# One scheduler task of six products where the second MLP layer had two tasks of three

## The chip, the cores and the metric

The kernel runs on one core of one Trainium2 chip. A core has a matrix engine (PE, with its weight loads listed apart as PEld), a vector engine (DVE), a scalar engine (ACT), a general engine (POOL) and a sequencer that mostly issues transfers (SP). Each engine works through its own instructions in the order in which they were written down, and waits for the others through semaphores. The metric is the time of one execution on the device in microseconds.

## The reference

Three stages follow each other. The attention works on 4 batches of 8 heads with 576 tokens of 64 numbers, under a mask of 64-token blocks. Its result is read as 2304 tokens of 512 numbers and goes through a two-layer MLP whose inner function is a leaky ramp with its own slope for each of 2048 hidden units. Then each token goes to one of 8 experts.

```python
x = attn_out.transpose(0, 2, 1, 3).reshape(2304, 512)
h = x @ w_in                                  # 512 -> 2048
g = np.maximum(h, 0.0) + alpha * np.minimum(h, 0.0)
y = g @ w_out                                 # 2048 -> 512
expert = np.argmax(y @ w_gate, axis=1)        # one of 8
out[mask] = gate_w[mask, None] * (np.maximum(y[mask] @ w1[e], 0.0) @ w2[e])
```

## The kernel before

All large products are made from numbers split into a high and a low part, so one product of the mathematics is three on PE: high by high, high by low and low by high.

**Attention** is cut into 16 pairs of heads (`pair`), each pair into 5 chunks of tokens (`unit`). For each chunk PE makes the scores `S`; DVE finds their maxima (`nb`, L428); ACT makes the exponentials `P` (L442); DVE their sums (`sm`, L449 and L450); POOL or DVE multiplies `P` by them (L477); PE transposes `P` into `PT` (L465); ACT or DVE copies that to `F` (L470); PE multiplies `F` with the values into `o` (L499), and the result goes to memory as `xT`. A pair begins with the transposes `tr` of its queries and keys (L340, L342), which ACT and DVE turn into `qhi`, `qlo`, `khi`, `klo` (L353 to L377). `tr`, `PT` and `o` of later pairs take turns in two PSUM buffers called `PT`, so a transpose waits until the readers of the one before the last are through.

**The first MLP** goes through the tokens in 9 groups of 256 (`Mlp1.plan`). For each of 16 slices `f` of the hidden units, `l1` makes 12 products of 256 columns into `l` (L578); DVE applies the ramp (`t`, L582 and L583), ACT casts the high part (`gh`, L586), POOL or DVE takes the low part (`gl`, L589). `l2` adds that slice into the two accumulators of the group, one for each 128 tokens, `acc` 0 and `acc` 1: three products of 512 columns each, `gh` by the high weights, `gh` by the low weights, and `gl` by the high weights (L609). When all 16 slices are in, ACT copies both accumulators to `y` (L620), and `route_plan` finds the expert of each token: transposes `rt`, products `lg`, a rank by the product `rk` (L723, L724), eleven small DVE operations that end in `ig` (L744), and two scatters of `info` that POOL issues one after the other (L747).

**Weights** of this MLP arrive as 64-bit numbers and are turned into high and low parts on the fly: ACT scales (L245), POOL takes the sign (L248), DVE puts the bits together (L251, L252), then the high part is cast (L256) and the low part is a difference (L260). While the last group runs, the weights of the first expert are loaded and split in the same way (`first_expert`, L1251 and L1256). The experts follow; the change does not touch them.

**What sets the order.** Attention, weights, MLP and routing are all tasks of one list scheduler (`Plan`). `order` simulates the engines with a duration given for each task. At each step it looks at all tasks whose inputs are there, takes those that can start within 100 ns of the earliest, and of these the one with the lowest priority number. A buffer is taken by the first task that uses it. The tasks' bodies are then written down in that order, and nothing reorders them later. `l1` and `l2` have numbers from 100000 up; attention has 0 to 16000, so attention goes first wherever both can start.

Of the kernel before, what the change touches and what calls it, by code (L numbers as in the profile page):

```python
# [18 lines left out]
P = 128  # L19
# [6 lines left out]
GT = 2  # L26
# [187 lines left out]
def cols(n):  # L214

    return max(n / 2.4 + 12, 108)
# [306 lines left out]
class Mlp1:  # L523
# [72 lines left out]
        
    def l2(A, pl, g, f):
        nc = A.nc
        for i in range(GT):
            acc = ("acc", g, i)  # L600
            if f == 0:
                pl.buf(acc, "H")
            c = slice(P * i, P * i + P)

            def second(on, i=i, c=c, acc=acc):
                wh, wl = (A.W["o", f][:, z] for z in range(2))
                gh, gl = pl["gh", g, f], pl["gl", g, f]
                for j, (x, w) in enumerate(((gh, wh), (gh, wl), (gl, wh))):
                    nc.tensor.matmul(pl[acc], lhsT=x[:, c], rhs=w, start=f == 0 and j == 0, stop=f == 15 and j == 2)  # L609

            pl.add(("PE", 3 * cols(512)), second, A.W1.names(("o", f)) + [("gh", g, f), ("gl", g, f)], [acc, ("l2", g, f)], 100000 + 100 * (16 * g + f + 1) + 20 + i)

    def fins(A, pl, g):
        nc = A.nc
# [208 lines left out]
class Experts:  # L823
# [132 lines left out]
    def tile128(A, n, W, it, x, step, aheads):  # L956
# [29 lines left out]
        step(1)  # L986
        Y = A.psp.tile("H", f"Y{n}")
        l2((0, 1))
        turn(1)
        aheads()  # L990
        step(7)
        l2(range(2, 8))
        nc.scalar.activation(A.yo[0], Y, AF.Copy, scale=it[:, 0, 1:2].bitcast(F32))
        A.scatter(A.yo[0], it)

    def tile64(A, n, W, it, x, step, aheads):
# [36 lines left out]
        for i in range(1, 4):  # L1033
# [3 lines left out]
            nc.scalar.copy(A.s, H)  # L1037
        Y = [A.psp.tile("H", f"Y{n}_{h}")[:, 0:256] for h in range(2)]
        l2(0, range(4))
        turn(3)  # L1040
        step(8)
# [290 lines left out]
```

## Time and profile before

| | us |
|---|---|
| median of 3 runs | 1041.59 |
| the three runs | 1037.69 to 1044.52 |
| profiled execution | 1040.76 |
| its span, first to last instruction | 1039.0 |
| PE busy | 934.6 (90% of the span) |
| DVE busy | 524.6 |
| ACT busy | 417.0 |
| POOL busy | 360.8 |

The span can be read in stages. Up to about 160 us attention, weight preparation and the first group run together, with DVE nearly as busy as PE. From there to about 519 us attention and MLP groups are interleaved, and PE is busy almost throughout. To about 716 us the MLP runs alone, and the experts end the kernel. PE has two clock levels, 2.4 GHz and 1.2 GHz; the profile lists the granted share (1.00 and 0.50). Matmuls are pipelined: the distance from one start to the next tells their cost better than their listed duration, which is longer. In the timeline a row merges equal instructions that follow each other; a bracket at its end holds the engine's idle time just before it and what ended it.

### The profile page before, as it was taken

How to read it: one execution, taken by the hardware profiler on the slowest of the kernel's cores; microseconds unless marked ns; L12 is line 12 of the kernel's file. 1: busy time of each engine (PE TensorE's matmuls, PEld its weight loads, DVE VectorE, ACT ScalarE, POOL GpSimd, SP SyncE). 2: the span in 40 equal slices, each digit the busy share in tenths (PEclk: the TensorE clock that was granted, in tenths of full speed). 3: DMA queues.
4: the chain of work that ended last, by engine and by line, in shares of the span. 5: the costliest groups of instructions: out<-in, count | busy, mean ns of one | idle time of the engine just before them, and what ended most of it. 6: DMA issues, size and time to landing. Idle time of an engine off the chain costs nothing. (4 is left out here: it accounts for less than half of the span.)

```text
span 1039.0 us, 18700 instructions
## 1 busy us (share of the span) xinstructions
PE 934.6 (90%) x6725; PEld 809.6 (78%) x6725; DVE 524.6 (50%) x1286; ACT 417.0 (40%) x1131; POOL 360.8 (35%) x429
## 2 busy tenths in 40 slices
PE   7884979999999999999999999998799999988554
PEld 6653868788788878888899999987688888877543
DVE  4898989554655645645443434455224314415130
ACT  5785554444544545545422121224124224325231
POOL 3556866332332333343322222232114212315030
PEclk8795998999899999999999999999999999999776
DMA  6553721112310121300010010033245212506110
GB/s 185 165 196 123 223 87 34 34 47 67 82 47 19 54 67 47 87 19 13 14 41 25 18 41 1 22 83 121 80 154 172 94 44 86 178 27 205 30 36 6
DMA packets 85296, 79.78 MB, mean 77 GB/s; under 512 B 53759, under 2 KB 65679, under 8 KB 85136
## 3 DMA queue, kind: packets, MB, share of 16 engines
q1 hardware_dynamic: 73984, 57.37, 19.0%
q0 software_dynamic: 4240, 11.56, 3.4%
q10 hardware_dynamic: 6912, 8.92, 2.4%
q8 instruction: 77, 1.26, 0.5%
q14 instruction: 83, 0.68, 0.2%
HBM read 63.49 MB, written 14.72 MB: 75 GB/s over the span
## 5 line engine op out<-in xcount | busy, mean ns | idle before, releaser
L578 PE MATMUL l<-xh,wi 128*128 128x256 f32 x1152 | 236.3, 290 | 1.9 <-DVE t L583 1.8
L578 PEld LDWEIGHTS l<-xh,wi 128*128 128x128 f32 x1152 | 191.6, 195 | 7.9 <-DVE t L583 2.7
L609 PE MATMUL acc<-wo,gh 128*128 128x512 f32 x576 | 191.7, 414 | 0.0
L578 PE MATMUL l<-xl,wi 128*128 128x256 f32 x576 | 165.3, 287 | 0.7 <-DVE xl L557 0.7
L589 POOL TENSOR_TENSOR gl<-t,gh 128x256 fp32r<-128x256 f32 x119 | 91.6, 770 | 193.9 <-ACT gh L586 163.0
L477 POOL TENSOR_SCALAR P<-P,sm 128x256 f32<-128x256 f32 (+4 forms) x89 | 102.2, 1152 | 162.4 <-DVE sm L450 70.2
L582 DVE TENSOR_SCALAR t<-l,al 128x256 f32<-128x256 f32 x144 | 69.5, 482 | 158.2 <-PE l L578 146.0
L586 ACT CAST gh<-t 128x256 fp32r<-128x256 f32 x144 | 58.5, 407 | 173.2 <-DVE t L583 75.5
L609 PE MATMUL acc<-wo,gl 128*128 128x512 f32 x288 | 113.9, 396 | 4.9 <-POOL gl L589 4.9
L578 PEld LDWEIGHTS l<-xl,wi 128*128 128x128 f32 x576 | 112.2, 195 | 4.6 <-DVE xl L557 1.3
L609 PEld LDWEIGHTS acc<-wo,gh 128*128 128x128 f32 x576 | 95.7, 190 | 16.1 <-issue 5.2
L465 PE MATMUL PT<-ident,P 128*128 128x128 f32 (+1 forms) x400 | 72.8, 297 | 27.3 <-DVE qlo L360 12.8
L470 ACT COPY F<-PT 128x256 f32<-128x256 f32 (+3 forms) x154 | 61.2, 415 | 74.3 <-PE PT L465 72.5
L465 PEld LDWEIGHTS PT<-ident,P 128*128 128x128 f32 (+1 forms) x400 | 48.7, 148 | 44.6 <-POOL P L477 10.9
L428 DVE TENSOR_REDUCE nb<-S 128x1 f32<-128x256 f32 (+4 forms) x160 | 70.9, 476 | 23.3 <-PE S L415 21.3
L499 PE MATMUL o<-F,v 128*64 128x128 f32 (+2 forms) x960 | 70.4, 279 | 2.3 <-ACT F L470 2.0
L609 PEld LDWEIGHTS acc<-wo,gl 128*128 128x128 f32 x288 | 54.3, 189 | 19.2 <-POOL gl L589 7.0
L442 ACT ACTIVATE P<-S,nb 128x128 f32<-128x128 f32 (+3 forms) x128 | 67.0, 532 | 5.6 <-DVE nb L428 3.0
L927 POOL DMA_INDIRECT out_dram<-yo,it x21 | 22.7, 1082 | 133.8 <-ACT yo L953 68.4
L499 PEld LDWEIGHTS o<-F,v 128*64 128x64 f32 (+1 forms) x960 | 50.0, 145 | 19.2 <-ACT F L470 5.5
L583 DVE SCALAR_TENSOR_TENSOR t<-l,t 128x256 f32<-128x256 f32 x144 | 61.1, 425 | 5.0
L880 DVE TENSOR_TENSOR e<-raw,e 128x512 fp32r<-128x512 f32 x44 | 39.8, 928 | 33.0 <-ACT e L879 33.0
(351 smaller groups left out, 1758.3 us busy)
## 6 DMA issues: line engine op xcount, KB each, us to landing
raw<-in_moe_w_dram SPq DMA_DIRECT2D x80, 256.0 KB
rawi<-in_moe_w_in_dram SPq DMA_DIRECT2D x16, 512.0 KB
rawo<-in_moe_w_out_dram SPq DMA_DIRECT2D x16, 512.0 KB
xr<-xT SPq DMA_DIRECT2D x9, 512.0 KB
v<-in_v_dram SPq DMA_DIRECT2D x32, 128.0 KB
x<-y ACTq DMA_DIRECT2D x16, 256.0 KB
xT<-xo ACTq DMA_DIRECT2D x16, 160.0 KB
q<-in_q_dram SPq DMA_DIRECT2D x20, 128.0 KB
```

The costliest lines, as they stand in the source:

```text
L428: nc.vector.tensor_reduce(pl["nb", p, c][:, j:j + 1], pl[Ss[j]][:, 0:N[j]], axis=AX.X, op=ALU.max, negate=True)
L442: nc.scalar.activation(pl[x][:, 0:N[j]], pl[Ss[j]][:, 0:N[j]], AF.Exp, bias=nb, scale=1.0, accum_out=pl["sm", p, c][:, j:j + 1])
L465: nc.tensor.transpose(pl[t][0:w, k], pl[x][:, P * k:P * k + w], A.K.ident)
L470: f(pl[F][:, 0:n], pl[t][:, 0:n])
L477: (nc.gpsimd if on == "POOL" else nc.vector).tensor_scalar(y, y, pl["sm", p, c][:, jj:jj + 1], None, op0=ALU.mult)
L499: nc.tensor.matmul(pl[o][r, 0:N], lhsT=v[0:w, 2 * kc + h], rhs=f, start=kc == 0, stop=kc == c, skip_group_check=True)
L578: nc.tensor.matmul(pl[l][:, 0:G], lhsT=a[:, c], rhs=b, start=k == 0 and j == 0, stop=k == 3 and j == 2)
L582: nc.vector.tensor_scalar(pl[t], x, 0.0, A.K.al[:, f:f + 1], op0=ALU.min, op1=ALU.mult)
L583: nc.vector.scalar_tensor_tensor(pl[t], x, 0.0, pl[t], op0=ALU.max, op1=ALU.add)
L586: nc.scalar.copy(pl[gh], pl[t])
L589: (nc.gpsimd if on == "POOL" else nc.vector).tensor_sub(pl[gl], pl[t], pl[gh].bitcast(F32))
L609: nc.tensor.matmul(pl[acc], lhsT=x[:, c], rhs=w, start=f == 0 and j == 0, stop=f == 15 and j == 2)
```

## The change

`l2` gave the scheduler two tasks for each slice, one for each half of the group's tokens; now it gives it one task that does the six products of both halves in a row. Products, operands, accumulators and their order within a slice stay the same. Both accumulators are now taken by the first such task of a group.

```diff
     def l2(A, pl, g, f):
         nc = A.nc
-        for i in range(GT):
-            acc = ("acc", g, i)
-            if f == 0:
+        accs = [("acc", g, i) for i in range(GT)]
+        if f == 0:
+            for acc in accs:
                 pl.buf(acc, "H")
-            c = slice(P * i, P * i + P)
-
-            def second(on, i=i, c=c, acc=acc):
-                wh, wl = (A.W["o", f][:, z] for z in range(2))
-                gh, gl = pl["gh", g, f], pl["gl", g, f]
+
+        def second(on):
+            wh, wl = (A.W["o", f][:, z] for z in range(2))
+            gh, gl = pl["gh", g, f], pl["gl", g, f]
+            for i, acc in enumerate(accs):
                 for j, (x, w) in enumerate(((gh, wh), (gh, wl), (gl, wh))):
-                    nc.tensor.matmul(pl[acc], lhsT=x[:, c], rhs=w, start=f == 0 and j == 0, stop=f == 15 and j == 2)
-
-            pl.add(("PE", 3 * cols(512)), second, A.W1.names(("o", f)) + [("gh", g, f), ("gl", g, f)], [acc, ("l2", g, f)], 100000 + 100 * (16 * g + f + 1) + 20 + i)
+                    nc.tensor.matmul(pl[acc], lhsT=x[:, P * i:P * i + P], rhs=w, start=f == 0 and j == 0, stop=f == 15 and j == 2)
+
+        pl.add(("PE", 6 * cols(512)), second, A.W1.names(("o", f)) + [("gh", g, f), ("gl", g, f)], accs + [("l2", g, f)], 100000 + 100 * (16 * g + f + 1) + 20)
```

Since one choice of the scheduler shifts all that follow, the order of the whole first 716 us differs from slice 7 of the first group on; before that point, and in the experts, it is the same. Of the 144 pairs of halves, 52 had other work between their halves; now none has. Stretches of other work (attention, routing) that stand between MLP tasks on PE are 153 after 167. Attention now reaches into the sixth group, where it ended with the fifth.

PE, slice 8 of the first group (`acc_0`, `acc_1` are the halves, `o_1` a chunk's product with the values). Before:

```order
L609 MATMUL acc_0_1521<-wo_1700,gh_8_1797 128x512 x2
L609 MATMUL acc_0_1521<-wo_1700,gl_8_1821 128x512
L499 MATMUL o_1_1860<-F_1_0_1817,v_1158 64x128
L499 MATMUL o_1_1860<-F_1_1_1844,v_1158 64x128
L499 MATMUL o_1_1860<-F_1_0_1817,v_1158 64x128
L499 MATMUL o_1_1860<-F_1_1_1844,v_1158 64x128
L609 MATMUL acc_1_1531<-wo_1700,gh_8_1797 128x512 x2
L609 MATMUL acc_1_1531<-wo_1700,gl_8_1821 128x512
```

And now:

```order
L609 MATMUL acc_0_1521<-wo_1700,gh_8_1797 128x512 x2
L609 MATMUL acc_0_1521<-wo_1700,gl_8_1821 128x512
L609 MATMUL acc_1_1525<-wo_1700,gh_8_1797 128x512 x2
L609 MATMUL acc_1_1525<-wo_1700,gl_8_1821 128x512
L499 MATMUL o_1_1867<-F_1_0_1817,v_1158 64x128
L499 MATMUL o_1_1867<-F_1_1_1844,v_1158 64x128
L499 MATMUL o_1_1867<-F_1_0_1817,v_1158 64x128
L499 MATMUL o_1_1867<-F_1_1_1844,v_1158 64x128
```

The halves stand together, and the attention product moves behind both.

DVE, a little later, about 150 us into the span before (`stw` and `wi` belong to the weights, `nb`, `nbb`, `P_3_1`, `qlo` and `klo` to attention). Before:

```order
L252 SCALAR_TENSOR_TENSOR stw_1988<-rawi_2_137,stw_1988 128x512
L428 TENSOR_REDUCE nb_4_2002<-S_4_1_1981 128x1
L433 TENSOR_TENSOR nbb_2027<-nb_4_2002 128x1
L360 SCALAR_TENSOR_TENSOR qlo_2029<-tr_0_1993,qhi_2014 128x512
L260 TENSOR_TENSOR wi_2_2018<-stw_1988,wi_2_2018 128x512
L362 TENSOR_TENSOR klo_2045<-tr_1_2005,khi_2023 128x512
L251 SCALAR_TENSOR_TENSOR stw_2034<-rawi_3_138,stw_2034 128x512
L252 SCALAR_TENSOR_TENSOR stw_2034<-rawi_3_138,stw_2034 128x512
```

And now:

```order
L252 SCALAR_TENSOR_TENSOR stw_1988<-rawi_2_137,stw_1988 128x512
L477 TENSOR_SCALAR P_3_1_1964<-P_3_1_1964,sm_3_1962 128x512
L428 TENSOR_REDUCE nb_4_2002<-S_4_1_1981 128x1
L260 TENSOR_TENSOR wi_2_2017<-stw_1988,wi_2_2017 128x512
L251 SCALAR_TENSOR_TENSOR stw_2024<-rawi_3_138,stw_2024 128x512
L252 SCALAR_TENSOR_TENSOR stw_2024<-rawi_3_138,stw_2024 128x512
L433 TENSOR_TENSOR nbb_2037<-nb_4_2002 128x1
L360 SCALAR_TENSOR_TENSOR qlo_2039<-tr_0_1993,qhi_2019 128x512
```

`qlo` has four more operations ahead of it: the scaling of `P_3_1`, which POOL did before, and three of the weights. `klo` goes far back.

POOL, around the scatters of the third group's routing, which run among the first slices of the fourth group (`gl_2` and `gl_3` are that group's; `q8hi`, `q8lo` are cleared for the next pair). Before:

```order
L477 TENSOR_SCALAR P_4_1_4819<-P_4_1_4819,sm_4_4809 128x320
L739 TENSOR_SCALAR ig_4888<-pid 128x2
L589 TENSOR_TENSOR gl_2_4905<-t_2_4867,gh_2_4897 128x256
L747 DMA info<-ig_4888,si_4883 18432x2 x2
L382 MEMSET q8hi_4970 64x64 x2
L382 MEMSET q8lo_4973 64x64 x2
L589 TENSOR_TENSOR gl_3_4990<-t_3_4948,gh_3_4979 128x256
```

And now:

```order
L739 TENSOR_SCALAR ig_4800<-pid 128x2
L477 TENSOR_SCALAR P_2_0_4759<-P_2_0_4759,sm_2_4760 128x384
L589 TENSOR_TENSOR gl_2_4823<-t_2_4770,gh_2_4788 128x256
L747 DMA info<-ig_4800,si_4795 18432x2 x2
L589 TENSOR_TENSOR gl_3_4865<-t_3_4837,gh_3_4845 128x256
L477 TENSOR_SCALAR P_3_1_4879<-P_3_1_4879,sm_3_4870 128x512
```

The low part of slice 3 stands directly behind the scatters, and a long scaling behind that. The routings of the fourth and fifth groups have this piece again.

## Rows read from the trace of the kernel before

**Rows 1.** Windows: length, busy us (count) of PE, PEld, DVE, ACT, POOL, PE clock, DMA.

```profile
240.00:280.00 40.00, 38.82 (x313) 32.33 (x310) 22.64 (x79) 20.97 (x72) 12.12 (x22) 0.87 0.28 75
360.00:400.00 40.00, 38.43 (x306) 32.64 (x304) 20.53 (x65) 17.81 (x59) 15.98 (x25) 0.96 0.19 44
560.00:600.00 40.00, 40.00 (x266) 36.68 (x266) 17.60 (x51) 8.87 (x22) 11.27 (x15) 1.00 0.09 27
680.00:720.00 40.00, 36.04 (x229) 32.19 (x227) 21.79 (x49) 13.28 (x29) 13.97 (x16) 1.00 0.42 116
```

**Rows 2.** Timeline of PE: start us, length us; halves of slices, whole and split.

```profile
125.50 0.61 PE L609 MATMUL acc<-wo,gh 128*128 128x512 f32 x2
126.19 0.61 PE L609 MATMUL acc<-wo,gh 128*128 128x512 f32 x2
...
226.10 0.73 PE L609 MATMUL acc<-wo,gh 128*128 128x512 f32 x2
...
226.99 0.50 PE L413 MATMUL S<-khi,qhi 64*128 64x512 f32 x2
...
227.91 0.73 PE L609 MATMUL acc<-wo,gh 128*128 128x512 f32 x2
...
228.71 0.49 PE L465 MATMUL PT<-ident,P 128*128 128x128 f32 x3
```

**Rows 3.** Timeline of PE, the stall of the first group and what follows.

```profile
154.38 2.29 PE L465 MATMUL PT<-ident,P 128*128 128x128 f32 x8 [3.82 <-DVE qlo L360]
...
159.70 0.58 PE L578 MATMUL l<-xh,wi 128*128 128x256 f32 x1
```

**Rows 4.** Timeline of DVE ahead of and behind `qlo`.

```profile
152.19 0.48 DVE L428 TENSOR_REDUCE nb<-S 128x1 f32<-128x320 f32 x1
...
153.55 0.68 DVE L360 SCALAR_TENSOR_TENSOR qlo<-tr,qhi 128x512 fp32r<-128x512 f32 x1
154.15 0.68 DVE L260 TENSOR_TENSOR wi<-stw,wi 128x512 fp32r<-128x512 f32 x1
...
155.35 0.68 DVE L251 SCALAR_TENSOR_TENSOR stw<-rawi,stw 128x512 int32<-128x512 int32 x1
156.06 1.41 DVE L252 SCALAR_TENSOR_TENSOR stw<-rawi,stw 128x512 int32<-128x512 int32 x1
```

**Rows 5.** Groups of instructions by line and shape: busy us, mean ns.

```profile
L477 DVE TENSOR_SCALAR P<-P,sm 128x512 f32<-128x512 f32 x17 | 9.1, 546 | 0.6
```

**Rows 6.** Windows as in Rows 1, three stretches at the lower clock.

```profile
153.20:163.40 10.20, 8.91 (x51) 7.84 (x52) 9.96 (x16) 5.87 (x15) 7.49 (x10) 0.50 0.26 59
259.00:269.30 10.30, 9.74 (x48) 8.30 (x49) 7.75 (x33) 4.81 (x15) 2.71 (x3) 0.50 0.22 64
375.10:378.50 3.40, 3.40 (x15) 3.12 (x13) 0.33 (x2) 1.15 (x5) 1.16 (x2) 0.50 0.09 13
```

**Rows 7.** Timeline of PE, fourth group, from the rank to slice 3.

```profile
361.12 0.38 PE L724 MATMUL rk<-oh,U 128*128 128x16 f32 x2
...
373.51 0.51 PE L609 MATMUL acc<-wo,gl 128*128 128x512 f32 x1 [1.22 <-POOL gl L589]
```

**Rows 8.** Timeline of POOL in the same stretch: the scatters, and slice 3.

```profile
365.30 1.06 POOL L747 DMA_INDIRECT info<-ig,si  x1 [1.35 <-DVE ig L744]
370.97 0.96 POOL L747 DMA_INDIRECT info<-ig,si  x1 [4.61 <-DMA info<-ig,si]
...
372.74 0.72 POOL L589 TENSOR_TENSOR gl<-t,gh 128x256 fp32r<-128x256 f32 x1
```

**Rows 9.** The scatters' line, all 18 of them.

```profile
DMA to landing us min/median/max: 3.3/3.6/5.4
```

**Rows 10.** Timeline of PE, an `l` block's starts, and the ninth group's stall.

```profile
120.31 0.40 PE L578 MATMUL l<-xh,wi 128*128 128x256 f32 x2
120.55 0.28 PE L578 MATMUL l<-xl,wi 128*128 128x256 f32 x1
...
686.86 0.50 PE L609 MATMUL acc<-wo,gl 128*128 128x512 f32 x1 [2.39 <-POOL gl L589]
```

**Rows 11.** Timelines of ACT and PE where the MLP ends.

```profile
715.12 2.19 ACT L1251 CAST e<-raw 128x512 fp32r<-128x512 f32 x4
...
722.34 1.27 PE L683 MATMUL rt<-ident,raw 128*128 128x128 f32 x8 [3.91 <-ACT raw L630]
```

**Rows 12.** The line of the accumulators' copies: who waited for it.

```profile
ACT F L470: 0.4, 1
```

## The prediction

> **What bounds the kernel now.** I read the windows first, 40 us at a time. Where the MLP runs alone PE is busy 40.00 of 40 us at full clock, with DVE, ACT and POOL under half; where attention is mixed in, it is busy 38.4 to 38.8 [rows 1]. PE is therefore the bound from about 160 us on, and a reordering that keeps its work can win only what PE loses: idle stretches, stretches at the lower clock, and whatever a change of work on PE costs. The timeline of PE shows few losses after 150 us. There is one wait of 3.82 us for `qlo` in the first group [rows 3]; waits of 1 to 2.4 us for a low part `gl` [rows 7, 10]; one of 3.91 us at the end of the MLP [rows 11]; and stretches at half clock, two of about 10 us and two of 3.4 us, of which the second stands at 463.8 and looks as the first [rows 6]. With half of the low-clock time all of it is about 26 us, 2.5% of the whole. The DVE timeline tells what the wait for `qlo` was [rows 4], the POOL timeline what the low parts waited for [rows 8].
>
> **The change, part by part.** Nothing is added or removed: all 864 products of L609 stay. What moves is the order, so each term below is a place where PE loses time, before and now.
>
> *Fewer changes of work on PE.* Whole halves start 126.19 - 125.50 = 0.69 us apart. A half that gives way to scores takes 226.99 - 226.10 = 0.89, and one that follows them 228.71 - 227.91 = 0.80 [rows 2]. So a stretch of other work costs 0.2 us where PE goes over to it and 0.1 where it comes back; for transposes I found nearer 0.1 in all. The order has 153 such stretches after 167, 14 fewer: at 0.1 to 0.3 each 1.4 to 4.2 us. I take **-3.0**; the ends are 0 (the pieces meet other expensive neighbours) and 52 split pairs by 0.2, -10.
>
> *The wait for `qlo`.* PE's transpose at 154.38 waits until DVE has read `tr` [rows 3]. In the order after DVE has four more operations ahead: the scaling of `P_3_1`, 0.55 us by the mean of its kind [rows 5], a low part, 0.68, and the two bit operations, 0.71 from start to start and 1.41 [rows 4]. That is 3.35 us. Some of the 1.36 us between 152.19 and 153.55 was itself waiting (the maximum takes 0.48), which the new operations fill: up to 0.8 comes off. `qlo` and the transpose are late by 2.5 us at best guess, and PE idles 6.3 instead of 3.82. What was queued behind it changes too: before, 5.3 us of attention at half clock followed, up to 159.70; now four `l` blocks do, and the attention comes later at full clock. DVE, not PE, sets the pace here, with as much to do as before, so I expect nothing back. **+2.5**; ends -1 (this attention at full clock takes about half of its 5.3 us, all of which is won, and `klo` is out of the way) and +5 (PE's longer idle stretch keeps the clock down for another 5 us).
>
> *Slice 3 behind the scatters.* In the fourth group the first scatter starts 4.2 us after the rank and the second 5.67 later, since POOL waits for the first to land; the low part is ready at 373.46, 12.3 us after the rank [rows 7, 8], because two clears stood in between. PE waited 1.22 us for it [rows 7], and again in the fifth group; each time the clock fell soon after for 3.4 us [rows 6], worth up to 1.7. So the pair of places cost 2 x 2.9 = 5.8. Now there are three. The clears are gone, so the low part is ready 4.2 + 3.9 + 0.96 + 0.72 = 9.8 us after the rank if the landing takes its median of 3.6, and 11.6 if 5.4 [rows 9]. PE wants it earlier: between rank and need stand scores of 512 columns (0.92 and 0.5 of changing over), two `l` blocks of 12 x 0.12 = 1.44 [rows 10], one whole pair, 1.4, six transposes, an `o` and two products, about 8.3 us. The wait is 1.5 us, 3.3 at the long landing. Three times 1.5, with the lower clock after every second one, is 7. **+1**; ends -5.8 (early landing, all gone) and +9 (3 x 3.3 + 3 x 1.7 - 5.8).
>
> *The second to third group.* Here only attention and routing can run, and the clock is low for 10.3 us [rows 6], worth up to 5. Now `P_3_1` stands behind these scatters on POOL, and PE wants it 5.2 us after the rank, where by the sum above the scatters alone end about 9 us after it. Either the clock falls as before and the wait hides in the slower products, or PE waits some 4 to 5 us at full clock. Both cost about what it costs now: **0**; ends -3 and +4.
>
> *The ninth group.* PE waits 2.39 us there already for a low part behind scatters [rows 10]. From rank to need it now has one `l` block (1.44) less and half a pair (0.69) more: **+0.8**; ends 0 and +1.
>
> *Into the experts.* ACT splits the expert's weights between its casts for the MLP; four of these stand in a row at 715.12, and PE waits 3.91 us for what ACT does after them [rows 11]. In the order after the first two of the four move ahead of the casts before them, so that their buffers come free, and the last loads start, 2 to 3 us sooner. If transfers set the pace, less is won: **-1.5**; ends -3 and 0.
>
> *Both accumulators at once.* The first product of a group now waits for two copies of L620 instead of one. PE never waited for either: the only one who did was ACT itself, 0.4 us once [rows 12]; an `l` block or transposes stand in between, after as before. **0**, with that cover. The Trainium skill speaks against it: the page "Perfetto Trace Analysis", section Optimizing Tensor Performance, asks that independent matmul groups rotate through different PSUM banks, so that emptying one overlaps the products of the next. By that rule the two halves, once separate, would now wait together at each border; rows and rule differ here, since no wait shows, and the rule's result stands below as a rival.
>
> The sum is -3.0 + 2.5 + 1 + 0 + 0.8 - 1.5 = -0.2. The profiled execution took 1040.76, 0.8 below the median of 1041.59, so the forecast is 1040.6, in round numbers **1041 us**: no change.
>
> **The rivals.**
>
> *Low parts behind scatters become the bound (slower).* For it: POOL holds every second scatter until the first has landed, 4.61 us [rows 8], the scheduler plans without that wait, and three groups now have a needed low part directly behind. Against it: before, the wait at PE came to 1.22. It decides if the landing takes 5.4 us each time and the clock then stays down 10 us, as after the 3.82 us wait, and not 3.4 [rows 6]: 3 x (3.3 + 5.1) - 5.8 = +19.4, with the rest of the sum at -1.2: 1059. Chance 0.10.
>
> *The bank rule holds (slower, but inside 1%).* If at each of the eight borders PE waited for the second copy, it would lose the copy and its semaphore, some 0.6 us: 8 x 0.6 = 4.8, 1045. The Trainium skill's sentence above is the reason to list it; the row of L620 speaks against it. Chance 0.05.
>
> *The losses vanish (faster).* Attention is spread over one more group, so PE has MLP work at hand more often. If the third group's low clock goes (-5), the low parts come in time (-5.8), the changes of work save 5 and the wait for `qlo` ends no later (0), with -1.5 at the end: -17.3 + 0.8 = -16.5, 1024. For it: the spread. Against it: in the order after the attention between second and third group is as long as before, and the low parts are wanted sooner. Chance 0.08.
>
> *Nothing but the changes of work.* 92 of 144 pairs were whole already, so the edit does little of what it says; if every stall merely moves, -3 is left: 1038. Chance 0.20.
>
> **How the numbers follow.** The forecast has the remaining 0.57. With its own ends weighed (they don't all fall together) it lies between 1034 and 1048. For 8 in 10 the range takes in the rivals inside 1% and part of the outer ones: **1032 to 1051**. One per cent, 10.4 us, is about what a measurement here can tell from no change. Slower by more needs the first rival, and a little of the forecast's upper end: 0.11. Faster by more needs the third: 0.09. No change: 0.80.
>
> **What would show it.** Right: L609 in groups of six without a break; PE's wait for `qlo` near 150 us grows to 5 to 7 us; a wait of 1 to 3 us for `gl` with L747 before it on POOL in three groups; the wait at the ninth group near 3; the one for L630 below 3.9; busy windows near 38.5 of 40 between 160 and 570. Wrong: if PE waits for `y`, if the clock is low for more than 45 us between 150 and 700 (27 now), or if a kind of wait not listed here stands in each group.

## The result, and the profile after

The changed kernel is **slower by 0.59%**: 1046.9 us against 1041.62 us in the same session, ratio 1.0059 with an interval of 1.0039 to 1.0078, some 6 us. The forecast was 1041, no change; the range (1032 to 1051) holds the time and it lies inside the 1% that I called no change, but the loss is measurable and my sum (-0.2) had none. The profiled execution took 1053.7 us, at the long end. A second one, of the same kernel run once more, took 1042.1, the shortest of its twelve; its trace stands beside the first where the two differ.

The windows show where to look. After, columns as in [rows 1]:

```profile
240.00:280.00 40.00, 36.38 (x286) 29.39 (x286) 20.86 (x73) 18.96 (x61) 11.76 (x20) 0.87 0.21 57
360.00:400.00 40.00, 38.58 (x306) 32.82 (x307) 23.11 (x67) 15.65 (x51) 13.76 (x18) 1.00 0.13 31
560.00:600.00 40.00, 39.02 (x278) 34.93 (x277) 16.66 (x51) 10.17 (x27) 11.58 (x15) 1.00 0.10 32
```

PE is busy 2.4 us less where the second group meets the third, and 1.0 us less at 560 to 600, where it had been busy without a gap [rows 1]; the stretch from 360 on did not get worse. The first contradicts my "busy windows near 38.5 of 40 between 160 and 570". The length of the MLP on PE is a yardstick from here on: from the first to the last start of an L609 product with `gh`, the two numbers ahead of the shapes at the end of the line. That line before, after, and in the second execution of after:

```profile
L609 PE MATMUL acc<-wo,gh x576: 387/396/628, 108.9 to 716.4; 128*128 128x512 f32 x192
```
```profile
L609 PE MATMUL acc<-wo,gh x576: 387/395/628, 110.3 to 725.8; 128*128 128x512 f32 x192
```
```profile
L609 PE MATMUL acc<-wo,gh x576: 387/395/505, 109.6 to 721.7; 128*128 128x512 f32 x192
```

That is 607.5 us before, 615.5 after and 612.1 in the second execution: the loss that both executions show is in the MLP. Behind it, up to the end of the span, the first takes 3.5 us more than before and the second 4.0 less, so what lies there differs more between two executions of one kernel than between the kernels. PE's four largest kinds of wait in this stretch (in all, times, longest), before:

```profile
PE acc L609 <- POOL gl L589: 4.9, 4, 2.4
PE PT L465 <- DVE qlo L360: 4.4, 2, 3.8
PE PT L465 <- POOL P L477: 3.3, 5, 1.2
PE l L578 <- DVE t L583: 1.8, 3, 1.1
```

And in the second execution of after:

```profile
PE acc L609 <- POOL gl L589: 6.7, 4, 2.2
PE PT L465 <- DVE qlo L360: 6.4, 1, 6.4
PE l L578 <- DVE t L583: 2.6, 4, 0.8
PE acc L609 <- POOL wo L260: 2.2, 2, 1.2
```

**The wait for `qlo`** came as the order said. PE and then DVE of after, answering to [rows 3, 4]:

```profile
157.69 1.08 PE L465 MATMUL PT<-ident,P 128*128 128x128 f32 x4 [6.39 <-DVE qlo L360]
```
```profile
153.32 0.47 DVE L477 TENSOR_SCALAR P<-P,sm 128x512 f32<-128x512 f32 x1
...
154.13 0.69 DVE L260 TENSOR_TENSOR wi<-stw,wi 128x512 fp32r<-128x512 f32 x1
154.75 0.68 DVE L251 SCALAR_TENSOR_TENSOR stw<-rawi,stw 128x512 int32<-128x512 int32 x1
155.46 1.41 DVE L252 SCALAR_TENSOR_TENSOR stw<-rawi,stw 128x512 int32<-128x512 int32 x1
...
156.87 0.68 DVE L360 SCALAR_TENSOR_TENSOR qlo<-tr,qhi 128x512 fp32r<-128x512 f32 x1
```

The scaling and the three operations of the weights stand ahead of `qlo`, and PE waits 6.39 us instead of 3.82: 2.6 more, where I had 2.5.

**Slice 3 of the fourth group** is late behind the scatters, as forecast. POOL and PE, answering to [rows 7, 8]:

```profile
363.29 1.05 POOL L747 DMA_INDIRECT info<-ig,si  x1 [1.35 <-DVE t L582]
367.13 0.96 POOL L747 DMA_INDIRECT info<-ig,si  x1 [2.80 <-PE o L499]
368.12 0.95 POOL L589 TENSOR_TENSOR gl<-t,gh 128x256 fp32r<-128x256 f32 x1
```
```profile
369.12 0.50 PE L609 MATMUL acc<-wo,gl 128*128 128x512 f32 x1 [1.42 <-POOL gl L589]
```

The second scatter starts 3.84 us after the first, the low part follows both, and PE waits 1.42 us for it, in three groups now. (The row of the second scatter names another releaser. By the trace the first scatter's transfer landed at 366.87, and in all nine groups the second scatter starts 0.26 to 0.27 us behind that landing.)

**Between second and third group** lies what I had put at nothing. PE from the last pair of the second group to the first `l` of the third, before and after:

```profile
254.44 0.60 PE L683 MATMUL rt<-ident,y 128*128 128x128 f32 x4
...
256.26 1.06 PE L687 MATMUL lg<-wg,xt 128*128 128x8 f32 x8 [0.33 <-ACT xt L646]
...
268.76 1.50 PE L465 MATMUL PT<-ident,P 128*128 128x128 f32 x8 [0.56 <-DVE qlo L360]
...
273.15 0.38 PE L578 MATMUL l<-xh,wi 128*128 128x256 f32 x1
```
```profile
251.14 0.39 PE L609 MATMUL acc<-wo,gl 128*128 128x512 f32 x1
251.46 0.39 PE L413 MATMUL S<-khi,qhi 64*128 64x256 f32 x2
...
264.31 1.51 PE L465 MATMUL PT<-ident,P 128*128 128x128 f32 x6 [1.16 <-DVE P L477]
...
270.75 0.63 PE L465 MATMUL PT<-ident,P 128*128 128x128 f32 x4 [0.82 <-ACT F L470]
...
272.82 1.09 PE L499 MATMUL o<-F,v 128*64 128x128 f32 x16 [1.00 <-ACT F L470]
273.85 0.39 PE L578 MATMUL l<-xh,wi 128*128 128x256 f32 x1
```

For 22.4 us (251.46 to 273.85) PE has nothing but attention and routing, whose steps wait for each other; before it was 18.7 (254.44 to 273.15). In the second execution it is 23.7. Not all of this is lost, since more attention is done there; what PE idles in it is 3.6 us in either execution (the three waits shown and two short ones), where it was 0.9. The first scores behind the last pair have 256 columns, those of `S_1`; before, `S_1` and `S_2` stood ahead of the last products and `S_3`, of 512 columns, came first behind them.

**A wait that was not there before** stands in the seventh, eighth and ninth group. PE of the seventh before, then PE and DVE after:

```profile
579.97 0.64 PE L609 MATMUL acc<-wo,gh 128*128 128x512 f32 x2
...
580.68 0.29 PE L723 MATMUL rk<-oh,ones 128*128 128x16 f32 x2
...
581.04 0.71 PE L609 MATMUL acc<-wo,gh 128*128 128x512 f32 x2
```
```profile
583.53 0.28 PE L578 MATMUL l<-xh,wi 128*128 128x256 f32 x1
583.65 0.29 PE L723 MATMUL rk<-oh,ones 128*128 128x16 f32 x2
...
584.92 0.39 PE L578 MATMUL l<-xh,wi 128*128 128x256 f32 x1 [0.76 <-DVE t L583]
```
```profile
584.44 0.42 DVE L583 SCALAR_TENSOR_TENSOR t<-l,t 128x256 f32<-128x256 f32 x1
```

The rank and the `l` blocks share two banks (tag `T`). The rank took the bank of `l_2`, so `l_4` must have that of `l_3`, which DVE reads until 584.86. Before, half a pair stood on either side of the rank and covered this; now `l_3`, rank and `l_4` follow each other. Against the start that `l_4` would have had, each such place costs some 0.9 us (the expectations below say 0.96); the profile lists 0.76 of it as idle.

**The clock.** Stretches of after at half clock, columns as above:

```profile
257.90:268.10 10.20, 9.04 (x41) 6.24 (x41) 5.29 (x26) 4.66 (x15) 1.87 (x2) 0.50 0.22 64
520.70:524.10 3.40, 3.40 (x17) 3.26 (x15) 1.07 (x3) 0.59 (x2) 0.82 (x1) 0.51 0.00 0
691.40:698.20 6.80, 6.15 (x25) 5.77 (x26) 0.91 (x2) 0.35 (x1) 1.27 (x2) 0.50 0.35 69
```

A fourth of 6.8 us follows the wait for `qlo`. The two of 3.4 us behind the old waits for low parts [rows 6] are gone; those at 520.7 and 691.4 stand behind waits for low parts of 1.62 and 2.70 us. In the second execution these two are missing and the one between the groups is 3.4 us longer, so that the MLP has 20.5 us at half clock instead of 27.3 and is 3.4 us shorter. Most of the 11.6 us between the two executions, 7.5, lies behind the MLP.

### The profile page after: what moved, and what is told of

It reads as the page before. It is cut to its first block, busy times and chain, and to the rows that moved or that the text cites. A ratio compares the mean times of both kernels' runs of the same rounds, so it can differ in the third digit from the quotient of the medians.

```text
span 1051.9 us, 18714 instructions
## 1 busy us (share of the span) xinstructions
PE 938.4 (89%) x6725; PEld 812.3 (77%) x6725; DVE 527.6 (50%) x1294; ACT 417.9 (40%) x1130; POOL 351.9 (33%) x422
## 5 line engine op out<-in xcount | busy, mean ns | idle before, releaser
L578 PE MATMUL l<-xh,wi 128*128 128x256 f32 x1152 | 238.9, 293 | 2.7 <-DVE t L583 2.6
L609 PE MATMUL acc<-wo,gh 128*128 128x512 f32 x576 | 188.0, 407 | 2.0 <-POOL wo L260 2.0
L589 POOL TENSOR_TENSOR gl<-t,gh 128x256 fp32r<-128x256 f32 x123 | 95.7, 779 | 224.4 <-ACT gh L586 199.1
L477 POOL TENSOR_SCALAR P<-P,sm 128x512 f32<-128x512 f32 (+4 forms) x78 | 90.6, 1165 | 151.3 <-DVE sm L450 45.9
L609 PE MATMUL acc<-wo,gl 128*128 128x512 f32 x288 | 114.0, 396 | 7.3 <-POOL gl L589 7.3
L609 PEld LDWEIGHTS acc<-wo,gh 128*128 128x128 f32 x576 | 99.4, 190 | 19.5 <-POOL wo L260 2.7
L609 PEld LDWEIGHTS acc<-wo,gl 128*128 128x128 f32 x288 | 54.3, 189 | 21.4 <-POOL gl L589 9.1
```

Source lines behind the costliest of these rows:

```text
L477: (nc.gpsimd if on == "POOL" else nc.vector).tensor_scalar(y, y, pl["sm", p, c][:, jj:jj + 1], None, op0=ALU.mult)
L578: nc.tensor.matmul(pl[l][:, 0:G], lhsT=a[:, c], rhs=b, start=k == 0 and j == 0, stop=k == 3 and j == 2)
L589: (nc.gpsimd if on == "POOL" else nc.vector).tensor_sub(pl[gl], pl[t], pl[gh].bitcast(F32))
L609: nc.tensor.matmul(pl[acc], lhsT=x[:, P * i:P * i + P], rhs=w, start=f == 0 and j == 0, stop=f == 15 and j == 2)
```

## The experiments

Ratios are to the kernel before in the same session. MLP is the length defined above, in one execution, and beside it what of it ran at half clock; the two change together from execution to execution.

| kernel | ratio (95%) | MLP us | half clock |
|---|---|---|---|
| before | 1 | 607.5 | 27.3 |
| changed | 1.0059 (1.0039 to 1.0078) | 615.5 | 27.3 |
| again | 1.005 (1.0029 to 1.0072) | 612.1 | 20.5 |
| joined | 1.0007 (0.9979 to 1.0035) | 604.6 | 17.1 |
| whole_late | 1.0028 (1.0 to 1.0056) | 606.8 | 23.9 |
| whole_early | 1.0045 (1.0021 to 1.0069) | 607.9 | 17.1 |
| rank_later | 1.0031 (1.0005 to 1.0057) | 608.5 | 20.5 |
| whole_mid | 0.9963 (0.9938 to 0.9988) | 601.6 | 17.1 |
| scatter_cost | 0.9926 (0.9895 to 0.9957) | 600.6 | 17.1 |
| all_three | 0.9886 (0.9845 to 0.9927) | 591.8 | 10.2 |
| halves_scatter | 0.9855 (0.9818 to 0.9891) | 591.5 | 10.2 |
| mid_scatter | 0.989 (0.9858 to 0.9921) | 592.2 | 6.8 |
| whole_first | 0.9908 (0.9874 to 0.9941) | 594.3 | 10.2 |
| whole_second | 0.9976 (0.9952 to 1.0) | 598.6 | 17.1 |
| joined_scatter | 0.9876 (0.9836 to 0.9915) | 594.6 | 6.8 |
| halves_scatter2 | 0.9866 (0.9828 to 0.9905) | 591.9 | 6.8 |

**1. again.** The changed kernel without an edit.

> The changed kernel once more, in the same session as the three that follow. Both theories: 5 to 7 us over the kernel before. It also gives a second trace: the waits of its plan (6.6 us for qlo near 151, 0.96 three times behind the rank for a T bank that L583 must read, 2.9 for the low part of the ninth group) should stand in it again within 0.3 us, while stretches at the low clock may move.

5.2 us over the kernel before. The waits of the plan stand where they stood, to 0.6 us (0.3 was expected; the ninth group's low part, 2.18 after 2.70, misses it); the clock's stretches moved. The loss is real, and belongs to the plan.

**2. joined.** The order of the kernel before, halves emitted together:

```diff
-                for j, (x, w) in enumerate(((gh, wh), (gh, wl), (gl, wh))):
-                    nc.tensor.matmul(pl[acc], lhsT=x[:, c], rhs=w, ...
+                for h, j, x, w in [(h, j, *z) for h in range(GT) if i == (f < 15) for j, z in enumerate(((gh, wh), (gh, wl), (gl, wh)))]:
+                    nc.tensor.matmul(pl["acc", g, h], lhsT=x[:, P * h:P * h + P], rhs=w, ...
```

> The plan of the kernel before, untouched, with the two halves emitted together at the place of the second half (of the first for f = 15). Theory A, the loss sits in the new places that replanning gave to attention, routing and scatters: the block of six is harmless, about 40 to 52 split pairs save their two changes of work, and no new wait comes: 3 to 6 us under the kernel before. Theory B, the block of six itself costs (no half is left to stand between two tasks that wait for each other, and both accumulators are held at once): 3 to 6 us over the kernel before, with waits at the places where a half stood between.

0.7 us over, with an interval from -2.2 to +3.6: neither theory's number. In the same session the changed kernel was 5.2 us over, so most of its loss is likely to come from the new places; up to 3.6 us by the block itself are not excluded. The gain of theory A did not come either.

**3 and 4. whole_late and whole_early.** Tasks of six in the last three groups, or in the first six (there the condition is `g >= 6`):

```diff
+        for part in [(0,), (1,)] if g < 6 else [(0, 1)]:
...
+            def second(on, part=part):
...
+            pl.add(("PE", 3 * len(part) * cols(512)), second, ...
```

> Tasks of six only in the last three groups, where the MLP runs alone; halves in the first six, whose order is that of the kernel before. Theory A with the pure groups as the place: two waits of 0.96 behind the rank (the seventh group has a pair there in this order), 0.3 to 0.5 more at the ninth group's low part, with the lower clock behind it in some executions: 2 to 5 us over the kernel before. If the mixed groups carry all of it: within 1 us of the kernel before.

2.9 us over, by an interval that begins at 1.0. The two waits behind the rank are there (0.76 us idle each), as expected; the ninth group's low part is waited for 2.17 us, not longer than before.

> Tasks of six only in the first six groups, halves in the last three. If the mixed groups carry the loss (qlo, the attention between second and third group, three low parts): 5 to 7 us over the kernel before. If the pure groups carry it: within 1 us of it, or 1 to 3 under it since the changes of work are saved here. Halved between both: 2 to 4 over.

4.7 us over, a little under the 5 to 7 expected. The `qlo` wait, the long stretch of attention and the three waits for low parts are in its trace, the T bank waits are not. Both places carry a part; how much each, these intervals don't say.

**5. rank_later.** The rank of the sixth to eighth group goes behind `l_4`:

```diff
-[("oh", g)], [rk], 0 if quick else 50000)
+[("oh", g)], [rk], 100000 + 1600 * (g + 1) + 450 if g >= 5 else 0)
```

> The changed kernel with the rank of the sixth to eighth group behind the block l_4 instead of ahead of it; nothing else moves but the scatters behind it by some 1.4 us. If the three waits of 0.96 us for the T bank are a loss of their own, they go: 2.9 us less than the changed kernel, 1 to 4 us over the kernel before. Rival: the wait only moves (rank or l_5 waits for L583 instead, or the low part of the ninth group, behind later scatters, is waited for longer): 4 to 7 us over the kernel before, as the changed kernel.

3.2 us over, and an MLP 3.6 us shorter than the changed kernel's at the same 20.5 us of half clock. PE at the same place, with two pairs behind the rank and no wait, and the low part of the ninth group:

```profile
584.45 0.29 PE L723 MATMUL rk<-oh,ones 128*128 128x16 f32 x2
...
584.81 0.70 PE L609 MATMUL acc<-wo,gh 128*128 128x512 f32 x2
...
691.45 0.50 PE L609 MATMUL acc<-wo,gl 128*128 128x512 f32 x1 [0.33 <-POOL gl L589]
```

The three waits are gone without another in their place at the rank, and the ninth group's wait shrank with them; a new wait for a low part, 0.42 us, stands at 594. By the trace the three waits were a loss of their own; the timing alone could not tell 3.2 from 5.2.

**6. whole_mid.** Tasks of six in the third to sixth group alone (`g < 2 or g >= 6` in the condition above).

> Tasks of six only in the third to sixth group; halves in the first two and the last three. Its order up to the third group is that of the kernel before, so the longer wait for qlo and the longer attention between second and third group cannot come. If these two carry the loss of the mixed groups: 1 to 4 us under the kernel before (changes of work saved, no new wait). Rival, every replanned mixed group loses, by low parts behind scatters: 2 to 5 us over it.

3.9 us faster than before. The same task that loses 5 us when it is everywhere gains 4 here: what it costs depends on its places. The gain need not be the changes of work that were expected to be saved: PE's waits of 1.1 to 1.2 us for low parts in the fourth and fifth group are gone too, down to one of 0.25, and the half-clock stretches behind them with them.

**7 and 8. scatter_cost and all_three.** The planner is told what POOL shows for the second scatter; and then also halves in the first two groups and the rank later:

```diff
-            pl.add(("POOL", 1100), lambda on, i=i: steps.scatter(i), ...
+            pl.add(("POOL", 3800 if i else 1100), lambda on, i=i: steps.scatter(i), ...
```

> The changed kernel, but the planner counts 3800 ns instead of 1100 for the second scatter, which is what POOL shows for it. If the waits for low parts (1.6 us three times, 2.4 to 2.9 at the ninth group) come from the planner not knowing that POOL waits for the first scatter's landing, they fall below 0.5 each: 4 to 7 us less than the changed kernel, within 2 us of the kernel before; qlo, the border between second and third group and the three waits of 0.96 stay. Rival: the low parts move to DVE and put its own work off (L582, qlo), and the sum stays: 4 to 7 us over the kernel before.

7.7 us faster than before, beyond what I expected. PE waits for no low part behind a scatter any more, the ninth group's included; in the order DVE has those low parts now. The wait for `qlo`, the long stretch between second and third group (23.5 us) and the three waits for the T bank are all still there.

> Halves in the first two groups, tasks of six from the third on, the rank of the sixth to eighth group behind l_4, and 3800 ns for the second scatter. If the four causes add up (no longer qlo wait and no longer border, no 0.96 waits, low parts in time, changes of work saved): 5 to 10 us under the kernel before. Rival, replanning trades each wait for another: within 2 us of the kernel before.

11.9 us faster, a little beyond the expectation.

**9 and 10. halves_scatter and mid_scatter.** The same cost in the kernel before; and with tasks of six in the third to sixth group.

> The kernel before, halves everywhere, with 3800 ns for the second scatter and nothing else. If it is the plan's ignorance of that wait, and not the length of the task, that costs the time: its order between second and third group has more of the attention done before the last products (S_4 instead of S_2 behind them), low parts come in time, so 7 to 11 us under the kernel before. Rival, the gain of the two kernels with this cost came from tasks of six: within 3 us of the kernel before.

15.1 us faster, beyond the 7 to 11 expected, and 13.9 in another session: the shortest time of all, without the change. Two of its windows:

```profile
240.00:280.00 40.00, 38.87 (x329) 33.17 (x327) 22.35 (x81) 20.70 (x69) 13.37 (x18) 1.00 0.33 84
360.00:400.00 40.00, 40.00 (x346) 33.94 (x344) 20.95 (x66) 19.37 (x68) 13.11 (x21) 1.00 0.22 58
```

The clock stays full where the second group meets the third, and the fourth group runs without a gap [rows 1]; the MLP is 16.0 us shorter than before.

> As the preceding one, with tasks of six in the third to sixth group alone. By the changes of work saved there it should be 1 to 3 us under it, 9 to 13 us under the kernel before. Rival, tasks of six gain nothing once low parts come in time: equal to the preceding one within 1 us.

11.5 us faster, not under the preceding one: no gain from tasks of six shows here.

**11 and 12. whole_first and whole_second.** Tasks of six in the first group alone, or in the second alone.

> The changed kernel's task in the first group alone, halves from the second on. The wait for qlo must be 6.6 us here too. Theory C, the attention-only stretch between second and third group is set by how far attention has come when the group's last products run, which any shift of the order changes: here S_4 stands behind the last products, so the stretch is under 10 us instead of 18.7, and the kernel 3 to 7 us under the kernel before in spite of qlo. Theory D, a longer task puts attention off, so the more tasks of six there are ahead of the border the longer the stretch: 20 us, and 2 to 5 us over the kernel before.

9.6 us **faster**, where 3 to 7 were expected. PE at the wait for `qlo`, and from the last pair of the second group to the first `l` of the third:

```profile
157.61 1.09 PE L465 MATMUL PT<-ident,P 128*128 128x128 f32 x4 [6.36 <-DVE qlo L360]
...
256.84 0.39 PE L609 MATMUL acc<-wo,gl 128*128 128x512 f32 x1
257.07 0.60 PE L683 MATMUL rt<-ident,y 128*128 128x128 f32 x4
...
264.27 0.36 PE L578 MATMUL l<-xh,wi 128*128 128x256 f32 x1
```

The wait of 6.36 us is there in full, and the kernel gains 9.6 us all the same. Only 7.2 us of attention (257.07 to 264.27) are left without cover, at full clock, where before 10.2 us ran at half clock. That is not all of the gain: the waits for low parts in the fourth and fifth group and the half-clock stretches behind them are gone as well. The length of the stretch speaks for theory C and against theory D; how much of the gain it is, this run does not tell.

> The changed kernel's task in the second group alone. qlo as in the kernel before (about 4 us). S_2 stands behind the last products as in the changed kernel, without its transposes of the step before. By theory C the stretch is between 18.7 and 22.4 us and the kernel 0 to 3 us over the kernel before; by theory D the same here, so it is the preceding kernel that tells them apart, and this one shows whether the second group's tasks alone bring the 3.7 us.

A miss for both theories: 2.5 us faster, at the edge of its interval. The stretch is 18.2 us, no longer than before, so the second group's tasks alone do not bring the 3.7 us. In these runs the long stretch stands only where both groups have tasks of six. Over all sixteen traces its length goes with the first scores behind the last pair: 7.2 to 8.6 us where only `S_4` is left, 18.2 to 18.9 where it is `S_2` or `S_3`, 22.4 to 23.7 where it is `S_1`; at half clock are 0, 6.8 to 10.2 and 10.2 to 13.7 us of them.

**13 and 14. joined_scatter and halves_scatter2.** The best plan, its halves emitted together as in 2, beside the plan itself.

> The plan of the kernel with halves and 3800 ns for the second scatter, untouched, with the two halves emitted together as in the joined kernel above. What is open: whether a block of six is worth anything by itself once the order stays. Theory A: some 40 to 50 split pairs save their changes of work, 2 to 4 us less than the same plan with halves, so 17 to 20 us under the kernel before. Theory B, each half was a filler that some other engine's result arrived behind: 1 to 4 us more than with halves.

> The kernel with halves everywhere and 3800 ns for the second scatter, once more in the same session as its joined form: 12 to 18 us under the kernel before.

12.9 and 13.9 us faster than before: no difference in time between them that the intervals would show. In the traces, at the same 6.8 us of half clock, the joined form's MLP is the longer one, 594.6 against 591.9. PE at one place where it loses, joined, and the same place with halves (from the trace of halves_scatter, the same kernel as halves_scatter2):

```profile
394.43 0.60 PE L342 MATMUL tr<-ident,k 128*128 128x128 f32 x4
395.33 1.09 PE L499 MATMUL o<-F,v 128*64 128x128 f32 x16 [0.29 <-ACT F L470]
```
```profile
389.20 0.60 PE L342 MATMUL tr<-ident,k 128*128 128x128 f32 x4
389.56 0.72 PE L609 MATMUL acc<-wo,gh 128*128 128x512 f32 x2
...
390.44 1.09 PE L499 MATMUL o<-F,v 128*64 128x128 f32 x16
```

With halves, 0.9 us of products stand between the transposes and the product that needs ACT's copy of them; joined, PE waits for the copy. Summed over the MLP, PE's idle times of more than 0.15 us are 11.8 us joined and 10.7 with halves, and the work between them is not less but 1.5 us more (reckoned as in the next section, 579.4 and 577.8). Theory A's saving does not show.

## Why the prediction was wrong, step by step

The measured terms are those of the second execution, whose MLP is 4.6 us longer than before. For both kernels the length of the MLP is taken apart in three: PE's idle times of more than 0.15 us; what the clock costs, put at half of the remaining time at half clock (an estimate); and the rest, which is the work at full clock with its changes.

| MLP, us | idle | clock | work |
|---|---|---|---|
| before | 15.3 | 12.8 | 579.3 |
| changed, first execution | 24.0 | 11.7 | 579.8 |
| changed, second execution | 23.5 | 8.0 | 580.6 |
| joined | 16.7 | 8.3 | 579.6 |

- **Fewer changes of work**, -3.0: measured +0.4 to +1.3. **This step failed.** The longer intervals of [rows 2] are there, but no time comes back when such places become fewer. The joined kernel has 122 stretches of other work where before has 167; at the forecast's 0.1 to 0.3 us each that would be 4.5 to 13.5 us, and neither its work (579.6 after 579.3) nor its time (0.7 us over) is less.
- **`qlo`**, +2.5: +2.6 by the row. Right, with the four operations named. But it decides nothing: whole_first has the same wait and is 9.6 us faster than before.
- **Slice 3**, +1: the three waits are there (1.42 us by the row, 1.5 forecast), 2.0 us more in all; the two low stretches behind the old ones, worth up to 3.4, went. About -1.4, inside its ends; in the first execution, where one such stretch came, about +0.4.
- **Second to third group**, 0: measured +2.7 of idle time, and in the second execution up to 1.7 more for the clock. **This step failed too**, in the overlap: I wrote that either the clock falls and the wait "hides in the slower products", or PE waits at full clock. The clock fell as before (10.2 and 13.7 us after 10.2), and PE waited besides. I also wrote that "in the order after the attention between second and third group is as long as before", having compared the steps around the scatters but not where the group's last products had moved. They now stand two scoring steps earlier (`S_1` and `S_2` come behind them), so more attention is left without cover. The `P_3_1` that I expected to be late was not what counted: it was ready at 270.06, and PE's transposes of it waited for ACT's copy until 270.61.
- **Ninth group**, +0.8: 2.70 against 2.39 in one execution, 2.2 in the other. About nothing, but for 6.8 us at half clock behind it in the first.
- **Into the experts**, -1.5: the wait for L630 is 3.14 and 2.9 instead of 3.91, so -0.8 to -1.0. Right in kind.
- **Both accumulators at once**, 0: PE waits 0.3 us for `y` once (the transposes of the routing, where nothing else was left to run), and in no group for the second copy. The Trainium skill's advice to rotate independent groups through different banks ("Perfetto Trace Analysis", section Optimizing Tensor Performance) is followed less than before, and the trace does not agree that this costs: no product of L609 waits for a copy at the borders.
- **Not in the sum at all:** the T bank behind the rank, 3 x 0.9 = +2.7, of which 2.3 is idle by the profile. **This term was missing.** I took the groups without attention as unchanged, because most of their pairs were whole. The half that stood on either side of the rank was the cover. This is the "kind of wait not listed" of my last paragraph, though in three groups and not in each, and rank_later takes it away. Also missing were two waits for `wo` in the first group, 2.2 us; they stand where before PE waited 1.9 us for `t` and `xl`, so they change little.

The idle time grew by 8.2 us: 2.6 at `qlo`, 2.0 at the low parts of slice 3, 2.7 between the groups, 2.3 at the T bank, and -1.4 in all the rest, where the wait of 1.19 us for a `P` at 203 us went. With -4.8 for the clock and +1.3 of work this makes the 4.6 us measured, to the rounding. That the first execution came out 8.0 us longer and the second 4.6 is mostly the clock: it costs 11.7 us in one and 8.0 in the other.

The range held the time by its width, since the sum was off in three places. The rivals: low parts as the bound came out below its price (their waits grew by 2 us, not 19), though they were worth more than I thought: in scatter_cost, where none is left, the idle time is 16.1 us instead of 23.5. The rival of the changes of work alone, 1038, fell with the first term. The losses did vanish, but in halves_scatter, by the cause that I had named for the slow side: the scheduler "plans without that wait". That is the larger lesson of the case.

What stays open: what each place is worth in the measured time, since most runs make a new order that differs in many places; and why the first group's shift alone leaves the border with only `S_4` to score, one step better than before, while the change in all groups leaves it two steps worse. The order shows it; no run here derives it from a rule. Nor is a difference between halves and tasks of six under the better plan settled beyond some 4 us (0.9855 to 0.989, intervals that overlap).

## What to carry to other kernels

Where a planner sets the order, price an edit by the places that move, and look first at the border where work runs out of cover: two scoring steps lost there left PE idle for 2.7 us more, and where one was won no half-clock time was left there. A price for a change of work, read at one place, is not a saving: with 45 such places fewer the kernel was no faster. A short task between two that depend on each other is cover; joining it to its twin can lay a wait bare. And give the planner the waits that the trace shows: one cost, from 1100 to 3800 ns, was worth 14 to 15 us and made the change needless.

## What the runs showed of the hardware

Two executions of the changed kernel put half-clock stretches at different places: after the wait for the ninth group's low part 6.8 us in one, none in the other; at the start of the experts 10.2 and 3.4 us. Its twelve executions in one session spread over 7 us. In halves_scatter, where PE idles for no more than 1.1 us at a time there, the clock is full from 163.5 to 706.3 us without a break; before, 17 us of that were at half. The second scatter of a group started 3.6 to 4.6 us after the first in all nine groups of the changed kernel, always just behind the first one's landing; before it was 3.8 to 5.7 us. The plan that counts 3800 ns for it left no wait for a low part behind a scatter in halves_scatter.
